# Nine warming matmuls instead of five, and the last stores cut at 80 rows and issued from two engines

## The chip, the core and the metric

The kernel runs on one NeuronCore of a Trainium2 chip. A core has engines with instruction streams of their own, which meet through semaphores: TensorE (PE; its weight loads are shown as PEld), VectorE (DVE), ScalarE (ACT), GpSimd (POOL) and SyncE (SP), which here only issues DMA. Sixteen DMA engines move data between HBM and the on-chip memory SBUF. Matmuls write PSUM, eight banks of 2 KB per partition, from which VectorE and ScalarE copy ("evict") results. The metric is device time of one execution in microseconds (us); lower is better.

## What is computed

The reference is a spectral layer followed by two gated feed-forward layers, on 2 x 3008 rows of 256 columns, all in float32:

```python
X = np.fft.rfft(x, axis=1)                      # x: (2, 3008, 256)
Yr = Xr @ w_r - Xi @ w_i + b_r
Yi = Xr @ w_i + Xi @ w_r + b_i
Yr, Yi = (np.sign(Y) * np.maximum(np.abs(Y) - 0.01, 0) for Y in (Yr, Yi))
y = np.fft.irfft(Yr + 1j * Yi, n=3008, axis=1)
x = y.reshape(6016, 256)
x = (sigmoid(x @ w_gate) * (x @ w_val)) @ w_out            # d_ff = 1536
x = (silu(x @ w2_gate) * (x @ w2_val)) @ w2_out            # d_ff = 1536
```

## The kernel before

**The whole.** The DFT of length 3008 = 47 x 64 is done as matmuls with tables, in stages: a first DFT over the 47 (94 rows with the two halves), a transposition, a second DFT over the 64, the complex product with w_r and w_i ("mix"), the shrinking, and the inverse in the same two steps. The two sequences (batches) are handled apart: batch 0 at the start of the kernel with everything kept on chip, batch 1 later, woven into the first feed-forward layer. The feed-forward layers run over 12 chunks of up to 512 rows and 12 blocks of 128 hidden columns; each float32 product there is made of three products of split operands (L636, L662). Weights come as float64 words and are split by VectorE and ScalarE as the kernel goes.

**The start.** `spectral_first` handles batch 0. Its function `load` (L288, L289) brings x in nine tiles `xr` of 94 partitions: two of 2 blocks ("tasks" `(0, 2)` and `(2, 2)`), seven of 4 blocks. Each tile takes two DMAs from SyncE, 80 rows and 14 rows. Six tiles have room at once, and the loads of the last three are issued when earlier tiles are used up. GpSimd fetches the table `f1f` (L293). Meanwhile VectorE clears a tile `idle`, and `warm(5)` issues five bf16 matmuls of 128 x 512 on it (L181), whose results nobody reads; each takes a PSUM tile of the pool `ps_b` (8 banks, tag "f"). Then the loop over the tasks: for each half d of the columns and each block a, one matmul of the tile's 94 x 128 block against `f1f` (L306, written into `p`); ScalarE (d = 0) and VectorE (d = 1) copy the bank into `zt`. With the last bank VectorE first converts the mixing weights `wmh` from `wraw` (L165, L166). PE takes its instructions in the order in which they are written, as does every other engine.

Then follows a loop over pairs of frequencies: `turn` transposes (L334, matmuls against the identity `eyes`) and copies out (ScalarE, L336), `forward` multiplies with a piece of the table `s2c` (L242), `mix` is 26 matmuls (L255), `inverse` uses pieces of `i1c` (L352). The pieces of `s2c` and `i1c` hold two turns each; the pieces 1 and 2 are loaded (L277) behind the first weights `raw` (L105 to L107).

**The queue of SyncE.** Nearly all loads and stores are issued by SyncE in program order. An issue also waits until the DMA that last used its semaphore has landed, so that about eight are under way. Around the change the order is: x tiles, `eyes` (L321), `s2c` piece 0, `wraw` (L154, L155), two bias rows (L156, L157), `f2s` (L158), `i1c` piece 0, weights, pieces 1 and 2.

**The end.** In the second layer, `turn_out` takes the finished chunk of up to 512 columns out of PSUM into `ot`, transposes it in blocks of 128 (L710) and copies each block into `ob` (ScalarE L716; VectorE L714 for the second block of the last chunk). Each row of `ob` is one row of the output, 1 KB. The rows of a block go to as many places as there are residues: a store (L721) ends where the block or a column of 94 rows of the output's layout ends. The last chunk has 384 rows and its stores are of 8, 94, 26 (first block), 68, 60 (second), 34 and 94 rows (third), all from SyncE. SyncE's last line, L860, waits for all DMAs to land.

The change touches `warm` and its call in `spectral_first`, and `turn_out`.

Of the kernel before, what the change touches and what calls it, by code (L numbers as in the profile page):

```python
# [9 lines left out]
F32 = mybir.dt.float32  # L10
# [10 lines left out]
PP = 32  # L21
NJ = 94
# [15 lines left out]
def tile_kernel(ctx, tc, x, w_r, w_i, b_r, b_i, wts, f1, f2, s2, i1, i1f, eye, one, out):  # L38
    nc = tc.nc
    P = 128  # L40
# [134 lines left out]

    idle = cp.tile([P, 512], BF16, name="idle")

    def warm(n):
        for i in range(n):
            pw = ps_b.tile([P, 512], F32, tag="f", name=f"warm{i}")  # L180
            nc.tensor.matmul(pw, idle[:, 0:P], idle, start=True, stop=True)  # L181


# [80 lines left out]
    def spectral_first(zz, ps):  # L264
# [3 lines left out]
        def bank(name):  # L268
            return ps.tile([P, 512], F32, tag="f", name=name)

        with tc.tile_pool(name="z0", bufs=1, reuse_waits="tile") as z0:
# [3 lines left out]
            def load_table2(c, t, src, into, bufs):  # L275
                into[c] = z0.tile([P, 4, P], F32, tag=t, bufs=bufs, name=f"{t}{c}")
                nc.sync.dma_start(into[c], src[:, 4 * c:4 * c + 4])  # L277

            tables = load_tables(z0)
            with tc.tile_pool(name="p1", bufs=1, reuse_waits="tile") as fp:  # L280
                xb = x[0].rearrange("(j p) c -> j p c", p=PP)
                xr = {}
                tasks = [(0, 2), (2, 2)] + [(p, 4) for p in range(4, PP, 4)]

                def load(t):
                    p0, n = tasks[t]
                    xr[t] = fp.tile([NJ, 4, 256], F32, tag="xr", bufs=6, name=f"xr0_{p0}")
                    nc.sync.dma_start(xr[t][0:80, :n], xb[0:80, p0:p0 + n, :])  # L288
                    nc.sync.dma_start(xr[t][80:94, :n], xb[80:94, p0:p0 + n, :])  # L289

                load(0)
                nc.gpsimd.memset(f1f[:, 96:P], 0.0)
                nc.gpsimd.dma_start(f1f[:, 0:96], f1[:, 2])  # L293
                for t in range(1, 6):
                    load(t)
                nc.gpsimd.memset(lam, -LAM)
                nc.scalar.activation(act, lam, AF.Sigmoid)
                nc.vector.memset(idle, 0.0)
                warm(5)
                next(tables)  # L300
                for t, (p0, n) in enumerate(tasks):
                    xt = xr.pop(t)
                    for d in range(2):
                        pt = bank(f"p1_0_{p0}_{d}")[:, :].rearrange("p (a c) -> p a c", c=P)
                        for a in range(n):
                            nc.tensor.matmul(pt[:, a], xt[:, a, d * P:(d + 1) * P], f1f,  # L306
                                             start=True, stop=True)
                        src = pt[:, 0:n, 0:96].rearrange("p a (q k) -> p k a q", q=4)
                        dst = zt[:, d, :, 4 * p0:4 * (p0 + n)].rearrange("p k (a q) -> p k a q", q=4)
                        if d and t == len(tasks) - 1:  # L310
                            next(tables)
                            nc.scalar.copy(dst[:, 0:KH // 2], src[:, 0:KH // 2])
                            nc.vector.tensor_copy(dst[:, KH // 2:], src[:, KH // 2:])
                        elif d:
                            nc.vector.tensor_copy(dst, src)
                        else:
                            nc.scalar.copy(dst, src)
                    if t + 6 < len(tasks):
                        load(t + 6)
                    if t == 3:  # L320
                        nc.sync.dma_start(eyes, eye)  # L321
                        load_table2(0, "s2c", s2, s2c, 3)
                        next(tables)
                        load_table2(0, "i1c", i1f, i1c, 4)
                        next(dec)
                next(tables)
# [258 lines left out]
    with tc.tile_pool(name="ps_b", bufs=8, space=PSUM) as ps_b:  # L585
        spectral_first(zz, ps_b)
        late_pools.append(ctx.enter_context(tc.tile_pool(name="wq", bufs=1, reuse_waits="tile")))
        mp = ctx.enter_context(tc.tile_pool(name="mp", bufs=2, reuse_waits="tile"))

        def split_x(m, ci):  # L590
            xs[m, ci] = tuple(mp.tile([P, 2, TC], F32R, tag=f"f{w}", bufs=RC, name=f"f{w}{m}_{ci}") for w in ("xh", "xl"))
            return xs[m, ci]

        def third_first():
            with tc.tile_pool(name="p3z", bufs=2, reuse_waits="tile") as fp:
                yield from stage3(0, fp, late_ps, zz, [split_x(0, c) for c in range(RC)], ps_b)
            pzs.close()

        third = third_first()
        next(third)  # L600
        fill(2)
        filled(2, nc.vector.tensor_copy)
# [48 lines left out]
    def project(m, ci, f, hh, hl):  # L651
        g0, tn = chunks[ci]
        wh, wl = blocks[m, f]
        first, last = runs[m, ci, f]
        if first:
            po[0] = [ps_o.tile([P, TC], F32, tag=f"o{d}", name=f"po{m}_{ci}_{d}") for d in range(2)]
        o = po[0]
        ops = [(d, w, v) for d in range(2) for w, v in ((wh, hh), (wh, hl), (wl, hh))]
        if (m, ci, f) == units[-1]:
            ops.sort(key=lambda op: op[2] is hl)  # L660
        for i, (d, w, v) in enumerate(ops):
            nc.tensor.matmul(o[d][:, :tn], w[:, 4 + d, :], v[:, :tn],  # L662
                             start=(first and d not in [q for q, _, _ in ops[:i]]),
                             stop=(last and d not in [q for q, _, _ in ops[i + 1:]]))
        if last and m:
            turned.append(turn_out(ci, o))
            next(turned[-1])
        if last and m == 0:
            drain(m, ci, f, o)
# [22 lines left out]
    def turn_out(ci, o):  # L692
        g0, tn = chunks[ci]
        end = ci == len(chunks) - 1
        ot = mp.tile([P, 2, TC], F32, tag="ot", bufs=1, name=f"ot{ci}")
        cut = 128 if end else tn
        for c in (slice(0, cut), slice(cut, tn)):
            if c.start < c.stop:
                nc.scalar.copy(ot[:, 0, c], o[0][:, c])
                nc.vector.tensor_copy(ot[:, 1, c], o[1][:, c])  # L700
        yield
        dst = out.rearrange("(b j p) c -> b p j c", b=B, p=PP)
        ob = mp.tile([P, 4, 256], F32, tag="ob", bufs=RC, name=f"ob{ci}")
        for j in range(0, tn, 256):
            pt = ps_f.tile([P, 2, 256], F32, tag="f", name=f"pt{ci}_{j}")
            js = [k for k in range(j, min(j + 256, tn), 128)]
            for a, k in enumerate(js):
                n = min(128, tn - k)
                for d in range(2):
                    nc.tensor.transpose(pt[:n, a, d * P:(d + 1) * P], ot[:, d, k:k + n], eyes)  # L710
            for a, k in enumerate(js):
                n = min(128, tn - k)
                if a and end:
                    nc.vector.tensor_copy(ob[:n, k // 128], pt[:n, a])  # L714
                else:
                    nc.scalar.copy(ob[:n, k // 128], pt[:n, a])  # L716
                r = 0
                while r < n:
                    pcol, jj = divmod(g0 + k + r, NJ)
                    step = min(n - r, NJ - jj)  # L720
                    nc.sync.dma_start(dst[pcol // PP, pcol % PP, jj:jj + step, :], ob[r:r + step, k // 128, :])  # L721
                    r += step
            yield


# [140 lines left out]
```

## Time and profile before

| | |
|---|---|
| median of 3 runs | 1378.81 us (1378.71 to 1380.22) |
| the profiled execution, its own time | 1378.57 us |
| its span, first to last instruction | 1376.5 us |
| PE busy | 1362.9 us, 99% |
| VectorE, ScalarE busy | 731.4 us (53%), 538.3 us (39%) |
| costliest line | L636, 3 x 1152 matmuls, 446.1 + 443.5 + 443.4 us |
| mean DMA rate | 55 GB/s; first of 40 slices 212 GB/s |

The span is what the trace covers; the time of an execution also holds what lies around it (here 2.07 us). A view of the trace gives start times in us from the span's start. "Busy" counts overlapping instructions of an engine once. In a timeline, consecutive instructions of one kind are merged into one row: start, time from the first's start to the last's end, and their number behind an x. SPq marks SyncE's issuing of DMAs: the row shows the issue, not the transfer. What an engine waited for stands behind "<-". DMA share is the busy time of the packets over that of 16 engines; it can exceed 1 where packets overlap. PEclk is the granted TensorE clock as a share of full speed.

### The profile page before, as it was taken

How to read it: one execution, taken by the hardware profiler on the slowest of the kernel's cores; microseconds unless marked ns; L12 is line 12 of the kernel's file. 1: busy time of each engine (PE TensorE's matmuls, PEld its weight loads, DVE VectorE, ACT ScalarE, POOL GpSimd, SP SyncE). 2: the span in 40 equal slices, each digit the busy share in tenths (PEclk: the TensorE clock that was granted, in tenths of full speed). 3: DMA queues.
4: the chain of work that ended last, by engine and by line, in shares of the span. 5: the costliest groups of instructions: out<-in, count | busy, mean ns of one | idle time of the engine just before them, and what ended most of it. 6: DMA issues, size and time to landing. Idle time of an engine off the chain costs nothing.

```text
span 1376.5 us, 16890 instructions
## 1 busy us (share of the span) xinstructions
PE 1362.9 (99%) x6784; PEld 1163.2 (85%) x6784; DVE 731.4 (53%) x1110; ACT 538.3 (39%) x941; POOL 11.0 (1%) x26
## 2 busy tenths in 40 slices
PE   9999999999999999999999999999999999999997
PEld 8998888888888888888889988888888888888896
DVE  1558984555334865633344755555455555555553
ACT  1655554444334443433333433333333333333332
POOL 1000000000000000000000000000000000000000
PEclk9999999999999999999999999999999999999999
DMA  8222442333332320200002101001101101100000
GB/s 212 67 78 83 147 127 82 108 108 103 100 110 80 100 77 0 77 31 31 1 27 77 50 1 31 24 7 32 31 1 31 32 0 31 31 6 26 27 16 12
DMA packets 57202, 76.35 MB, mean 55 GB/s; under 512 B 6084, under 2 KB 40615, under 8 KB 57124
## 3 DMA queue, kind: packets, MB, share of 16 engines
q1 hardware_dynamic: 54980, 71.69, 17.0%
q0 software_dynamic: 2144, 3.58, 1.3%
q8 instruction: 53, 0.87, 0.3%
q14 instruction: 25, 0.20, 0.0%
HBM read 51.53 MB, written 23.72 MB: 55 GB/s over the span
## 4 chain that ended last, share of the span: by engine, by line
PE 97%; DMA 1%; DVE 1%; ACT 0%; SPq 0%; issue 0%; ACTq 0%
PE pg L636 56%; PE po L662 28%; PE pm L255 5%; PE p L501 2%; PE p L306 2%; PE p L242 1%; PE pi L352 1%; PE pt L710 1%; PE p L219 1%; PE pi L448 1%; PE p L490 1%; PE pt L334 0%; DMA xr<-in_x_dram 0%; DMA xin<-xT 0%; PE p1e L577 0%; DVE yl L440 0%
## 5 line engine op out<-in xcount | busy, mean ns | idle before, releaser
L636 PE MATMUL pg<-fxh,wh 128*128 128x512 f32 (+1 forms) x1152 | 446.1, 387 | 0.0
L636 PE MATMUL pg<-fxl,wh 128*128 128x512 f32 (+1 forms) x1152 | 443.5, 385 | 0.0
L636 PE MATMUL pg<-fxh,wl 128*128 128x512 f32 (+1 forms) x1152 | 443.4, 385 | 0.0
L640 ACT ACTIVATE sg<-pg 128x512 f32<-128x512 f32 (+1 forms) x288 | 169.6, 589 | 362.2 <-PE pg L636 361.6
L644 DVE TENSOR_TENSOR h<-sg,pg 128x512 f32<-128x512 f32 (+1 forms) x288 | 194.5, 675 | 188.8 <-ACT sg L640 183.7
L647 ACT CAST hh<-h 128x512 fp32r<-128x512 f32 (+1 forms) x288 | 176.6, 613 | 300.2 <-DVE h L644 299.2
L649 DVE TENSOR_TENSOR hl<-h,hh 128x512 fp32r<-128x512 f32 (+1 forms) x288 | 195.9, 680 | 154.7 <-ACT hh L647 152.3
L636 PEld LDWEIGHTS pg<-fxh,wl 128*128 128x128 f32 x1152 | 216.2, 188 | 41.4
L636 PEld LDWEIGHTS pg<-fxh,wh 128*128 128x128 f32 x1152 | 216.5, 188 | 41.0 <-DVE fxl L512 0.2
L636 PEld LDWEIGHTS pg<-fxl,wh 128*128 128x128 f32 x1152 | 216.4, 188 | 39.9 <-issue 0.2
L662 PE MATMUL po<-hh,wh 128*128 128x512 f32 (+1 forms) x576 | 223.6, 388 | 0.3 <-ACT hh L647 0.3
L662 PE MATMUL po<-hh,wl 128*128 128x512 f32 (+1 forms) x576 | 221.9, 385 | 0.0
L662 PE MATMUL po<-hl,wh 128*128 128x512 f32 (+1 forms) x576 | 221.6, 385 | 0.0
L642 DVE TENSOR_TENSOR sg<-sg,pg 128x512 f32<-128x512 f32 (+1 forms) x144 | 97.4, 676 | 157.9 <-ACT sg L640 157.7
L662 PEld LDWEIGHTS po<-hh,wl 128*128 128x128 f32 x576 | 108.1, 188 | 20.8
L662 PEld LDWEIGHTS po<-hh,wh 128*128 128x128 f32 x576 | 108.2, 188 | 20.5 <-ACT hh L647 0.6
L662 PEld LDWEIGHTS po<-hl,wh 128*128 128x128 f32 x576 | 108.2, 188 | 20.2 <-DVE hl L649 0.2
L255 PE MATMUL pm<-wmh,Xh 128*128 128x256 f32 x192 | 54.2, 282 | 0.9 <-DVE Xl L234 0.9
L255 PE MATMUL pm<-wmh,Xl 128*128 128x256 f32 x192 | 53.7, 280 | 0.0
L255 PE MATMUL pm<-wml,Xh 128*128 128x256 f32 x192 | 53.7, 280 | 0.0
L625 DVE TENSOR_TENSOR fxl<-xin,fxh 128x512 fp32r<-128x512 f32 (+1 forms) x44 | 28.5, 677 | 19.4 <-ACT fxh L624 19.2
L255 PEld LDWEIGHTS pm<-wmh,Xh 128*128 128x128 f32 x192 | 36.2, 188 | 3.1 <-DVE Xl L234 2.7
(103 smaller groups left out, 854.2 us busy)
## 6 DMA issues: line engine op xcount, KB each, us to landing
raw<-in_moe_w_gate_dram SPq DMA_DIRECT2D x24, 256.0 KB
raw<-in_moe_w_val_dram SPq DMA_DIRECT2D x24, 256.0 KB
raw<-in_moe_w_out_dram SPq DMA_DIRECT2D x24, 256.0 KB
xin<-x2T SPq DMA_DIRECT2D x11, 512.0 KB
xT<-xo SPq DMA_DIRECT2D x26, 188.0 KB
x2T<-xo SPq DMA_DIRECT2D x9, 512.0 KB
xin<-xT SPq DMA_DIRECT2D x8, 512.0 KB
i1s<-in_tab_i_dram POOLq DMA_DIRECT2D x12, 256.0 KB, 4.2
```

Source lines behind the costliest of these rows:

```text
L219: nc.tensor.matmul(pt[c][:96], f1s[:, w, :], v, start=(i == 0), stop=(i == 2))
L255: nc.tensor.matmul(pm[:, k, :], a, w, start=(j == 0), stop=(j == len(ops) - 1))
L306: nc.tensor.matmul(pt[:, a], xt[:, a, d * P:(d + 1) * P], f1f, start=True, stop=True)
L501: nc.tensor.matmul(pt[:, d, q * NJ:(q + 1) * NJ], z[:, q, d * P:(d + 1) * P], f2s, start=True, stop=True)
L625: nc.vector.tensor_tensor(xl[:, k, :tn], xin[:, k, :tn], xh[:, k, :tn], op=ALU.subtract)
L636: nc.tensor.matmul(pg[:, s, :tn], w[:, 2 * s + k, :], v[:, k, :tn], start=(i == 0), stop=(i == 5))
L640: nc.scalar.activation(sg[:, :tn], pg[:, 0, :tn], AF.Sigmoid)
L642: nc.vector.tensor_tensor(sg[:, :tn], sg[:, :tn], pg[:, 0, :tn], op=ALU.mult)
L644: nc.vector.tensor_tensor(h[:, :tn], sg[:, :tn], pg[:, 1, :tn], op=ALU.mult)
L647: nc.scalar.copy(hh[:, :tn], h[:, :tn])
L649: nc.vector.tensor_tensor(hl[:, :tn], h[:, :tn], hh[:, :tn], op=ALU.subtract)
L662: nc.tensor.matmul(o[d][:, :tn], w[:, 4 + d, :], v[:, :tn], start=(first and d not in [q for q, _, _ in ops[:i]]), stop=(last and d not in ...
```

## The change

`warm` gets a second argument: the first `banks` matmuls take a new PSUM tile each, later ones write again into the last tile taken. The call becomes `warm(9, 5)`: nine matmuls, five tiles, as many tiles as before.

In `turn_out`, stores of the last chunk (`end`) take at most 80 rows each. A store is put into the list `late` and, outside the last chunk, taken out and issued from SyncE at once, as before. In the last chunk the stores of its first block (k = 0) and those of more than 60 rows are issued from SyncE at once; the others stay in the list and are issued from ScalarE at the end of the last block. With the sizes above that makes, in order, 8, 80, 14, 26, 68, 80 rows from SyncE and 60, 34, 14 rows from ScalarE.

```diff
--- before.py
+++ after.py
@@ -175,9 +175,10 @@
 
     idle = cp.tile([P, 512], BF16, name="idle")
 
-    def warm(n):
+    def warm(n, banks):
         for i in range(n):
-            pw = ps_b.tile([P, 512], F32, tag="f", name=f"warm{i}")
+            if i < banks:
+                pw = ps_b.tile([P, 512], F32, tag="f", name=f"warm{i}")
             nc.tensor.matmul(pw, idle[:, 0:P], idle, start=True, stop=True)
 
 
@@ -296,7 +297,7 @@
                 nc.gpsimd.memset(lam, -LAM)
                 nc.scalar.activation(act, lam, AF.Sigmoid)
                 nc.vector.memset(idle, 0.0)
-                warm(5)
+                warm(9, 5)
                 next(tables)
                 for t, (p0, n) in enumerate(tasks):
                     xt = xr.pop(t)
@@ -701,6 +702,7 @@
         yield
         dst = out.rearrange("(b j p) c -> b p j c", b=B, p=PP)
         ob = mp.tile([P, 4, 256], F32, tag="ob", bufs=RC, name=f"ob{ci}")
+        late = []
         for j in range(0, tn, 256):
             pt = ps_f.tile([P, 2, 256], F32, tag="f", name=f"pt{ci}_{j}")
             js = [k for k in range(j, min(j + 256, tn), 128)]
@@ -717,9 +719,14 @@
                 r = 0
                 while r < n:
                     pcol, jj = divmod(g0 + k + r, NJ)
-                    step = min(n - r, NJ - jj)
-                    nc.sync.dma_start(dst[pcol // PP, pcol % PP, jj:jj + step, :], ob[r:r + step, k // 128, :])
+                    step = min(n - r, NJ - jj, 80 if end else NJ)
+                    late.append((dst[pcol // PP, pcol % PP, jj:jj + step, :], ob[r:r + step, k // 128, :]))
+                    if not end or k == 0 or step > 60:
+                        nc.sync.dma_start(*late.pop())
                     r += step
+            if j + 256 >= tn:
+                for pair in late:
+                    nc.scalar.dma_start(*pair)
             yield
```

## Rows read from the trace of the kernel before

**Rows 1.** The page: PE's totals (busy us, share, instructions) and the granted clock in 40 slices
```profile
PE 1362.9 (99%) x6784; PEld 1163.2 (85%) x6784; DVE 731.4 (53%) x1110; ACT 538.3 (39%) x941; POOL 11.0 (1%) x26
...
PEclk9999999999999999999999999999999999999999
```

**Rows 2.** Chain of waits, 0 to 36 us: start us, us, what
```profile
8.28 24.25 PE p L306 x112
```

**Rows 3.** Timeline of PE, 22.7 to 41.8 us: start us, us, engine, line, what
```profile
22.71 9.81 PE L306 MATMUL p<-f1f,xr 94*128 94x128 f32 x45
32.31 0.42 PE L334 MATMUL pt<-eyes,zt 128*128 128x128 f32 x1
32.92 1.76 PE L334 MATMUL pt<-eyes,zt 128*128 128x128 f32 x7 [0.20 <-ACT zt L312]
34.50 1.67 PE L242 MATMUL p<-s2c,z 128*128 128x128 f32 x8
36.01 0.60 PE L334 MATMUL pt<-eyes,zt 128*128 128x128 f32 x4
36.44 1.06 PE L242 MATMUL p<-s2c,z 128*128 128x128 f32 x8
...
40.92 1.06 PE L242 MATMUL p<-s2c,z 128*128 128x128 f32 x8
```

**Rows 4.** Timeline of PE, 0 to 10 us; in brackets the idle time before
```profile
1.19 2.31 PE L181 MATMUL warm<-idle 128*128 128x512 bf16 x5 [1.19 <-DVE idle L298]
4.22 3.75 PE L306 MATMUL p<-f1f,xr 94*128 94x128 f32 x16 [0.71 <-DMA f1f<-in_tab_f_dram]
8.28 2.05 PE L306 MATMUL p<-f1f,xr 94*128 94x128 f32 x8 [0.31 <-DMA xr<-in_x_dram]
```

**Rows 5.** Timeline of the end, 1365 to 1377 us
```profile
1366.78 0.65 ACT L716 COPY ob<-pt 128x256 f32<-128x256 f32 x2 [0.75 <-PE pt L710]
1367.17 2.39 SPq L721 DMA_DIRECT2D out_dram<-ob  x7
1367.18 0.42 DVE L714 COPY ob<-pt 128x256 f32<-128x256 f32 x1 [0.89 <-ACT ob L716]
```

**Rows 6.** Windows: us, busy of each engine, then PEclk, DMA share, GB/s
```profile
8.00:12.00 4.00, 3.72 (x17) 3.75 (x18) 0.36 (x1) 0.48 (x1) 0.00 (x0) 1.00 1.21 240
25.00:30.00 5.00, 5.00 (x26) 5.00 (x25) 1.42 (x4) 0.48 (x1) 0.00 (x0) 1.00 0.98 337
30.00:35.00 5.00, 4.80 (x22) 4.18 (x22) 2.43 (x7) 1.67 (x4) 0.00 (x0) 1.00 0.03 12
1371.00:1373.00 2.00, 0.00 (x0) 0.00 (x0) 0.00 (x0) 0.00 (x0) 0.00 (x0) 0.50 0.15 43
1373.00:1375.00 2.00, 0.00 (x0) 0.00 (x0) 0.00 (x0) 0.00 (x0) 0.00 (x0) 0.50 0.13 47
1375.00:1376.50 1.50, 0.00 (x0) 0.00 (x0) 0.00 (x0) 0.00 (x0) 0.00 (x0) 0.50 0.00 0
```

**Rows 7.** Timeline of SyncE's issues, 11 to 26 us
```profile
14.16 0.36 SPq L321 DMA_DIRECT2D eyes<-in_tab_eye_dram  x1
...
15.65 0.38 SPq L154 DMA_DIRECT2D wraw<-in_w_r_dram  x1
...
17.45 0.64 SPq L156 DMA_DIRECT2D braw<-in_b_r_dram  x1
...
19.12 0.34 SPq L158 DMA_DIRECT2D f2s<-in_tab_f_dram  x1
...
23.53 0.43 SPq L277 DMA_DIRECT2D s2c<-in_tab_s_dram  x1
```

**Rows 8.** SyncE's waits, 0 to 32 us: total us, times, longest us
```profile
SPq L158 <- DMA xr<-in_x_dram: 0.5, 1, 0.5
```

**Rows 9.** DMA issues of the end, 1360 to 1377 us
```profile
out_dram<-ob SPq DMA_DIRECT2D x2, 94.0 KB
```

**Rows 10.** DMA issues of 0 to 30 us: KB each, us to landing
```profile
f1s<-in_tab_f_dram POOLq DMA_DIRECT2D x1, 70.5 KB, 9.3
```

## The prediction

> **What bounds the kernel now.** I read the page's totals first, then the chain of waits over the first 36 us, then TensorE's (PE's) timeline there, SyncE's issues beside it, and last the end. The totals say that PE is busy for 1362.9 of 1376.5 us [rows 1]: only 13.6 us are idle, and a change that fills idle time can't give more. But busy time is not work done. The chain spends 24.25 us, from 8.28 us on, in one line, the 112 recorded passes of the first DFT stage, `p` at L306 [rows 2]. Each matmul of 128 columns shows as two passes there.
>
> What the reader is to see next is the distance from one matmul to the next, which tells the clock's level here. In `p` 45 passes fill 22.71 to 32.31 us, where L334 begins: 9.60 / 45 = 0.213 us from start to start. The transposes L334 behind it take (34.50 - 32.92) / 7 = 0.226 us each, and from 36.01 us on the same transposes take (36.44 - 36.01) / 4 = 0.108 us [rows 3]. The factor of two is that between TensorE's levels of 1.2 and 2.4 GHz. So everything up to some 35 us ran at 1.2 GHz. The page's granted clock prints 9, full, from the first slice on [rows 1]; it does not show this, and the spacing decides. What PE did before: five warming matmuls in 2.31 us (512 columns at 1.2 GHz are 0.427 us), an idle gap of 0.71 us until f1f is there, and 28 us of `p` on 94 partitions, short of gaps [rows 4]. None of that raised the clock; it rose, between 34.5 and 36 us, in work on all 128 partitions with gaps in it [rows 3].
>
> Behind 36 us PE has hardly a gap until the end, so what is gained ahead of it reaches the end whole. At the end, the last seven stores are issued within 2.39 us from 1367.17 us [rows 5], yet the span ends at 1376.5. From 1371 to 1375 us the DMA share is 0.15 and 0.13 of 16 engines, so about two engines work and fourteen stand idle [rows 6].
>
> **The change part by part.**
>
> *Warming, if the clock rises.* Nine matmuls at 1.2 GHz start at 1.19 us and stream until 1.19 + 0.40 + 8 x 0.427 = 5.0 us, without the gap at 3.5 to 4.2: unbroken work on all 128 partitions, where the work that raised the clock later had gaps [rows 3]. Their banks are touched by PE alone, so none of them waits. I take it that the clock is up by the time `p` has been going a little. Then `p` is bound by its input. The third tile of x arrives at about 8.2 us [rows 4]. The later ones can be read off SyncE, whose issues wait for them: L321 at 14.16 us, L154 at 15.65, L156 at 17.45, L158 at 19.12 [rows 7, 8] stand for tiles six to nine of nine; the 14 rows that are loaded apart come some 0.2 us later. A tile of 16 passes takes 16 x 0.11 = 1.76 us instead of 16 x 0.213 = 3.41, about what a tile takes to arrive. From tile six: 14.4 + 4 x 1.76 = 21.4 us, against 32.3 now [rows 3]: **-10.9 us**. The exact moment of the rise hardly matters so long as it lies before 8.2 us.
>
> Behind it, sixteen passes of L334 and L242 that now run at half rate save 0.1 us each, 1.6 us; ScalarE's evictions between them hide part, so 0.5 to 1.6, and I take the middle, **-1.1**. What is late next is the tables: the third L242 group would come at 40.92 - 12.0 = 28.9 us [rows 3], and its table is issued at 23.53 us, first of the last four of 256 KB [rows 7]. DMA is full until 30 us and empty after [rows 6]; at 337 GB/s three tables take 2.3 us, so this one's bytes come at about 28 us and its landing is known a little later. A stall of 0 to 1.5 us; I take **+0.5**. The tables' bytes and the weights' beside them are moved no later than now. Sum **-11.5** (-12.5 to -9.5).
>
> *Warming, if it does not rise.* `p` starts 0.8 us later; the wait of 0.31 us for the third tile takes part of it back [rows 4]: **+0.4** (0.3 to 0.8).
>
> *Stores.* Chunks other than the last are issued as before. In the last, the two stores of 94 rows of 1 KB [rows 9] become 80 + 14. SyncE issues 8, 80, 14, 26, 68 and 80 rows; ScalarE, with nothing else left to do, issues 60, 34 and 14 after its last copy at 1367.4 us; its first waits for VectorE's copy until 1367.6 [rows 5]. From 1371 to 1375 us two engines move 45 KB per us, so each takes 0.045 us a row [rows 6]. A 94-row store leaves 47 rows to each of the two. As 80 rows over sixteen engines it leaves 5, and the 14 add one: the x loads, cut at 80 in the same way, hold the share at 1.21 [rows 6]. So 2 x (47 - 6) = 82 rows less on each of the two engines, 82 x 0.045 = **-3.7 us**. Bounds: at best the last issue decides, six of seven of 2.39 us, 1369.2 us, with the few tenths to its first packet and the 1.5 us that now lie between the last packet and the end [rows 6], which would be some -5; at worst nothing, if two engines have to carry it all the same. The stores of 34 and 68 rows stay as they are.
>
> ScalarE issues no DMA in this trace. Three issues cost it 1.0 us at SyncE's 0.34 each (2.39 / 7), up to 2 us at twice that: done at 1368.6 to 1369.6, no later than SyncE's own last. I take nothing for it.
>
> The Trainium skill, DMA: Bandwidth & Descriptors, "Rules for kernel authors", speaks against this part: spreading transfers over several issuing engines, or cutting one into parts by partitions, brings no bandwidth, as all run on the same sixteen DMA engines. By it the stores' term would be 0 and the sum 1367.3 us. The trace bears it out only where the sixteen are busy, and here two are.
>
> *Sum.* The profiled execution took 1378.57 us, 2.07 us more than its span and 0.24 us below the median of 1378.81. 1378.57 - 11.5 - 3.7 = 1363.4; with 0.2 for the median, **1363.6 us**.
>
> **The rivals.**
>
> *The clock stays low, or falls back.* For it: 24 us of gapless `p` have not raised it, and the five did not. Against: both were less than unbroken work on all partitions. It could also rise and fall again: at the upper level the first two tiles are done by 6.8 us and PE idles until 8.2 for the third [rows 4]; `p` then runs at 1.2 GHz as now. The only fall that the trace shows is after PE's last matmul, 0.50 from 1371 us on [rows 6]. Either way only the stores gain: 1378.8 + 0.4 - 3.7 = **1375.5 us**. Chance 0.30 (no rise 0.18, fall 0.12). The Trainium skill, TensorE: Matmul & The Clock Gate, "HAM oscillation", describes such a fall for a kernel whose PE waits for DMA between bursts; no run here shows one in the middle of a kernel.
>
> *The tail stays as long*, since the few engines carry the pieces too or the last landing has another cause: with the clock up 1367.3 us, chance 0.04; with the clock down 1379.2 us, no change, chance 0.03, which is also what it gives if the change does nothing that it says.
>
> *Slower: ScalarE's first DMA.* It has issued none before, and a queue used for the first time may answer slowly. The slowest landing among the early ones is 9.3 us (POOL's f1s, behind a full queue) [rows 10]. Its third, issued at 1369.0 where each issue takes twice SyncE's time, would land at 1378.3 instead of 1375.4, +2.9; with the clock down and 0.4 for the later `p`, 1378.8 + 0.4 + 2.9 = **1382.1 us** (with the clock up it would still be faster). From a landing of 6 us on it decides, from 8.8 us on measurably. Against it: DMA is nearly idle there. Chance 0.03.
>
> **How the numbers follow.** Forecast 0.60, rivals 0.30, 0.07 and 0.03. A measurement of this kernel can tell about 0.2%, 2.8 us, from no change, so faster begins below 1376.05. The forecast with its bounds spans 1360.5 to 1367; the first rival, 1374 to 1376.3, has 0.30 and must be in. So the range is 1360.5 to 1376.3, and 0.12 is left out. Faster: 0.60 + 0.04 + 0.7 of 0.30 (1375.5 is close to the bound) = 0.85. Same: 0.09 + 0.03 = 0.12. Slower 0.03. The likeliest case's own range is 1360.5 to 1367.
>
> **What would show it.** Right: passes of L306 at 0.11 us instead of 0.213, PE waiting for x at L306 again and again, L334 beginning near 21.4 us; at the end last packets near 1371.3 us of the old clock, DMA share well above 0.15 while they run. Wrong on the clock: L306 at 0.213 us from 8.3 us on, L334 near 32.7 us. Wrong on the stores: a stretch of several us at two engines, or a wait of SyncE's last line for ScalarE's stores. The forecast as a whole falls if the time is not below 1370 us.

## The result, and the profile after

The changed kernel takes 1364.33 us (median of nine runs, 1363.77 to 1376.53), the kernel before 1379.13 us (median of nine). The ratio is 0.9902, with a 95% interval of 0.9883 to 0.992. Eight of the nine runs lie between 1363.77 and 1366.31 us, one at 1376.53. In two of the experiments below (e4, e9) one run each had a mean granted clock near 0.56 and took about 2280 us; those two are left out of every number here. The profiled execution took 1366.31 us, 2 us more than the median; the waits in its middle are shown further down.

The page's totals, of which the first line stands here with the span, and the granted clock in 40 slices:

```profile
span 1364.3 us, 16902 instructions
...
PE 1352.1 (99%) x6788; PEld 1150.6 (84%) x6788; DVE 731.0 (54%) x1110; ACT 537.2 (39%) x941; POOL 11.0 (1%) x26
...
PEclk9999999999999999999999999999999999999999
```

PE is busy for 10.8 us less (1362.9 to 1352.1) with four more instructions [rows 1]. It did no less work; it did the same work at a higher clock. The clock row looks the same as before and again shows nothing of that.

PE's timeline from 0 to 36 us (start us, us, engine, line, what; in brackets the idle time before and what ended it), where the kernel's L306, L334 and L242 are now L307, L335 and L243:

```profile
1.19 4.02 PE L182 MATMUL warm<-idle 128*128 128x512 bf16 x9 [1.19 <-DVE idle L299]
5.00 2.67 PE L307 MATMUL p<-f1f,xr 94*128 94x128 f32 x16
8.50 13.45 PE L307 MATMUL p<-f1f,xr 94*128 94x128 f32 x112 [0.83 <-DMA xr<-in_x_dram]
21.79 0.27 PE L335 MATMUL pt<-eyes,zt 128*128 128x128 f32 x1
...
24.58 0.60 PE L335 MATMUL pt<-eyes,zt 128*128 128x128 f32 x4
...
30.23 1.13 PE L243 MATMUL p<-s2c,z 128*128 128x128 f32 x8 [0.57 <-DMA s2c<-in_tab_s_dram]
```

`p` begins at 5.00 us, without a gap behind the nine warming matmuls, where it waited 0.71 us before [rows 4]. (A row's end is modelled, so the warming row reaches 5.21.) The first 16 passes take 2.67 us instead of 3.75, so the clock rose inside them; the 112 behind take 13.45 us instead of 24.25 [rows 2]. L335 begins at 21.79 us, where L334 began at 32.31 [rows 3]. PE now waits 0.83 us for the third tile of x, and 0.57 us for the table of the third L243 group, which comes at 30.23 us instead of 40.92.

The chain of waits over the same stretch (start us, us, what) has changed its kind:

```profile
2.50 5.59 DMA xr<-in_x_dram
...
8.17 7.74 DMA xr<-in_x_dram
...
16.36 6.38 DMA wraw<-in_w_i_dram
...
24.20 5.90 DMA s2c<-in_tab_s_dram
```

Loads stand in the chain of the first 30 us now, where `p` did [rows 2]. It ends in PE's wait for the table at 30.23 us, so a still faster PE would bring nothing there, and an earlier table no more than the wait of 0.57 us. `p` itself is close to both bounds, the arrival of x and PE's own pace. Its sixth tile begins at 14.57 us, and the 64 passes from there to L335 take 7.22 us, 0.113 us each; that is about PE's own pace at the high clock, which e10 below shows: 112 passes from 15.06 to 27.57 us without a wait, 0.112 us each.

PE's waits over the whole span (total us, times, longest us) show where some of the gain is given back:

```profile
PE pm L256 <- DVE Xl L235: 1.5, 1, 1.5
PE p L502 <- DMA z<-scr: 1.2, 1, 1.2
```

The first is 0.9 us in the kernel before, the second has no counterpart there. Both lie far behind the start, at 253 and 349 us.

The end, in the timeline and in windows (us; busy us of PE, PEld, DVE, ACT, POOL; PEclk; DMA share; GB/s):

```profile
1358.69 0.65 ACT L718 COPY ob<-pt 128x256 f32<-128x256 f32 x2 [0.74 <-PE pt L712]
1359.09 2.27 SPq L725 DMA_DIRECT2D out_dram<-ob  x6
...
1359.37 1.41 ACTq L729 DMA_DIRECT2D out_dram<-ob  x3
```

```profile
1360.00:1361.00 1.00, 0.00 (x0) 0.00 (x0) 0.00 (x0) 0.00 (x0) 0.00 (x0) 1.00 0.48 142
1361.00:1362.00 1.00, 0.00 (x0) 0.00 (x0) 0.00 (x0) 0.00 (x0) 0.00 (x0) 0.79 0.46 128
1362.00:1363.00 1.00, 0.00 (x0) 0.00 (x0) 0.00 (x0) 0.00 (x0) 0.00 (x0) 0.50 0.36 115
1363.00:1364.30 1.30, 0.00 (x0) 0.00 (x0) 0.00 (x0) 0.00 (x0) 0.00 (x0) 0.50 0.00 0
```

ScalarE's last copies begin at 1358.69 us, 8.1 us earlier than in the kernel before [rows 5]. From there to the span's end (called the tail from here on) it takes 5.6 us, where it took 1376.5 - 1366.78 = 9.7. SyncE issues six stores in 2.27 us, ScalarE three in 1.41 (0.47 each, waits included). ScalarE's come in the order 34, 60, 14 rows and not 60, 34, 14; by the sizes in the trace its first issue, at 1359.37 us, is of 34 rows. The stretch of 4 us at a share of 0.13 to 0.15 [rows 6] is gone; the share stays at 0.36 to 0.48 until the last packets.

So of the 12.2 us between the two spans (1376.5 - 1364.3), 8.1 come from before the last copies and 4.1 from the tail.

### The profile page after: what moved, and what is told of

It is laid out like the page before. It is cut to its first block, busy times and chain, and to the rows that moved or that the text cites. A ratio compares the mean times of both kernels' runs of the same rounds, so it can differ in the third digit from the quotient of the medians.

```text
span 1364.3 us, 16902 instructions
## 1 busy us (share of the span) xinstructions
PE 1352.1 (99%) x6788; PEld 1150.6 (84%) x6788; DVE 731.0 (54%) x1110; ACT 537.2 (39%) x941; POOL 11.0 (1%) x26
## 4 chain that ended last, share of the span: by engine, by line
PE 91%; DMA 4%; DVE 2%; ACT 1%; SPq 1%; issue 0%; DVEq 0%; ACTq 0%
PE pg L637 53%; PE po L663 27%; PE pm L256 5%; PE p L502 2%; PE p L243 1%; DMA raw<-in_moe_w_out_dram 1%; DMA xr<-in_x_dram 1%; PE pi L353 1%; DMA xin<-xT 1%; PE pt L712 1%; PE p L220 1%; PE p L491 1%; PE pi L449 0%; DMA wraw<-in_w_i_dram 0%; DMA s2c<-in_tab_s_dram 0%
## 5 line engine op out<-in xcount | busy, mean ns | idle before, releaser
L256 PE MATMUL pm<-wmh,Xh 128*128 128x256 f32 x192 | 54.2, 282 | 1.5 <-DVE Xl L235 1.5
L256 PE MATMUL pm<-wmh,Xl 128*128 128x256 f32 x192 | 53.7, 280 | 0.0
L256 PE MATMUL pm<-wml,Xh 128*128 128x256 f32 x192 | 53.7, 280 | 0.0
L256 PEld LDWEIGHTS pm<-wmh,Xh 128*128 128x128 f32 x192 | 36.2, 188 | 3.6 <-DVE Xl L235 3.2
```

The lines of the kernel that those rows point to most:

```text
L256: nc.tensor.matmul(pm[:, k, :], a, w, start=(j == 0), stop=(j == len(ops) - 1))
```

## The experiments

Each kernel was timed beside the kernel before, and the ratio is to that. Rows carry the line numbers of the run that they come from: where an edit adds lines they stand a little further (e10's L310 is L307). A run's tail comes from its one profiled execution. The fences of edits show the lines that differ, without those around them; a longer gap is marked by dots. The theory: the clock's early rise brings some 11 us, the shorter tail some 4, each without the other. The rivals were that one of the two carries it all, that the warming matmuls are paid for, and that the tail is a matter of the issuing engine.

| run | edit | median us (runs) | ratio, 95% interval | tail us |
|---|---|---|---|---|
| e1 | warming alone | 1369.08 (4) | 0.9921 (0.9906 to 0.9936) | 9.9 |
| e2 | stores alone | 1376.11 (6) | 0.9971 (0.9959 to 0.9982) | 5.6 |
| e3 | stores cut, all from SyncE | 1364.76 (4) | 0.9887 (0.987 to 0.9903) | 6.4 |
| e4 | stores not cut, two from ScalarE | 1369.11 (3) | 0.9913 (0.9897 to 0.993) | 9.6 |
| e5 | seven warming matmuls | 1374.87 (12) | 0.9941 (0.9917 to 0.9965) | 5.7 |
| e6 | twelve warming matmuls | 1364.39 (4) | 0.9889 (0.9876 to 0.9901) | 5.7 |
| e7 | nine, and four in the wait for x | 1364.39 (4) | 0.989 (0.9877 to 0.9903) | 5.7 |
| e8 | nine on 94 partitions | 1376.07 (6) | 0.9973 (0.9961 to 0.9984) | 5.7 |
| e9 | third tile of x late | 1383.03 (7) | 1.0026 (1.0015 to 1.0038) | 5.7 |
| e10 | the same, wait filled | 1369.99 (3) | 0.9936 (0.9914 to 0.9959) | 5.7 |
| e11 | stores cut at 47 rows | 1376.5 (1) | | 16.6 |
| e12 | twelve, 68 and 34 rows cut | 1364.46 (4) | 0.9896 (0.9879 to 0.9912) | 5.4 |

### One part of the change without the other: e1 and e2

```diff
 e1 = the kernel before, and
-    def warm(n):
+    def warm(n, banks):
 ...
-                warm(5)
+                warm(9, 5)
 e2 = the changed kernel, and
-                warm(9, 5)
+                warm(5, 5)
```

> Nine warming matmuls, stores as before. Theory (the clock's early rise is worth some 11 us, the stores some 4): 1368 to 1369 us in nearly all runs, L306 at 0.11 us per pass from some 6.5 us on, the tail from PE's last matmul to the end 9.7 us as before. Rival (the stores carry the gain, or both are needed): over 1375 us.

> Five warming matmuls, stores as changed. Theory: the clock stays low until the transposes, 1374.5 to 1375.5 us, the tail some 5.5 us instead of 9.7. Rival (the tail belongs to ScalarE's issues and ends no earlier without them in the right place, or the gain was one of the clock alone): 1378 to 1380 us.

e1 keeps the long tail of 9.9 us and is 0.8% faster; e2 has the short tail and is 0.3% faster. The two reductions, 0.79% and 0.29%, make 1.08%, against 0.98% (0.8 to 1.17) for the change as a whole: the parts add up. e2's median lies 0.6 us above the expected range; its batch's kernel before stood at 1380.52 us, 1.4 above the other batch. In e2's trace PE's timeline has `p` at the low clock to the end:

```profile
8.28 24.23 PE L307 MATMUL p<-f1f,xr 94*128 94x128 f32 x112 [0.22 <-DMA xr<-in_x_dram]
32.30 0.42 PE L335 MATMUL pt<-eyes,zt 128*128 128x128 f32 x1
```

These are the 24.25 us and 32.31 us of before [rows 2, 3].

### What in the stores shortens the tail: e3, e4, e11, e12

```diff
 e3: all from SyncE
-                    if not end or k == 0 or step > 60:
+                    if True:
 e4: not cut
-                    step = min(n - r, NJ - jj, 80 if end else NJ)
+                    step = min(n - r, NJ - jj, NJ)
 e11 = e3, cut at 47 rows
-                    step = min(n - r, NJ - jj, 80 if end else NJ)
+                    step = min(n - r, NJ - jj, 47 if end else NJ)
```

> Nine warming matmuls; the last stores cut at 80 rows, all nine issued from SyncE in the order of the rows. Theory (it is the 94 rows that lie on two DMA engines): most of the tail's gain stays; SyncE has three more issues of some 0.34 us behind its six, so the last one comes 1.0 us later and the tail is 5.9 to 6.7 us instead of 5.5; 1364.5 to 1365.5 us. Rival (the second issuing engine brings the gain): tail over 8 us, 1367 to 1368.5 us.

> Nine warming matmuls; the last stores not cut, those of 60 and 34 rows issued from ScalarE. Theory: two stores of 94 rows still put 47 rows each on two DMA engines, tail 8.5 to 9.7 us, 1367 to 1368.5 us. Rival (the second issuing engine brings the gain): tail near 5.5 to 6.5 us, 1364 to 1365.5 us.

> Nine warming matmuls; the last stores cut at 47 rows instead of 80 (94 = 47 + 47), all issued from SyncE. Theory (the number of rows of a store decides over how many DMA engines it spreads, and 47 does worse than 94): a long stretch at a DMA share below 0.13, tail over 9 us. Rival (shorter stores are faster, whatever their number of rows): tail 7 us or less, about as with the cut at 80 from SyncE alone.

The cut alone (e3) brings the tail to 6.4 us, the second issuer alone (e4) to 9.6, next to nothing. Both together bring 5.6. Thus in the traces the cut is worth 3.3 of the 4.1 us and ScalarE's issues, where the cut has made room for them, 0.8. The medians show the cut as well (1364.76 us in e3 against 1369.08 in e1) and nothing for the second issuer alone (1369.11 in e4); one of e4's three runs took 1366.68 us, and why is not known. They don't resolve the 0.8 us. e3's timeline shows what they save, nine issues from one engine in 3.38 us against 2.27:

```profile
1357.10 3.38 SPq L725 DMA_DIRECT2D out_dram<-ob  x9
```

In e4 two issuers are at work, and the windows still have the long stretch near two of sixteen engines (a share of 0.125):

```profile
1362.00:1364.00 2.00, 0.00 (x0) 0.00 (x0) 0.00 (x0) 0.00 (x0) 0.00 (x0) 0.50 0.18 63
1364.00:1366.00 2.00, 0.00 (x0) 0.00 (x0) 0.00 (x0) 0.00 (x0) 0.00 (x0) 0.50 0.11 39
```

e11, of which there is one run, decides what the cut does. It makes the stores shorter than the change does, and the tail is 16.6 us, the longest of all. Its issues and windows:

```profile
1358.56 8.11 SPq L725 DMA_DIRECT2D out_dram<-ob  x11
```

```profile
1366.00:1368.00 2.00, 0.00 (x0) 0.00 (x0) 0.00 (x0) 0.00 (x0) 0.00 (x0) 0.50 0.07 24
1368.00:1370.00 2.00, 0.00 (x0) 0.00 (x0) 0.00 (x0) 0.00 (x0) 0.00 (x0) 0.50 0.07 24
1370.00:1372.00 2.00, 0.00 (x0) 0.00 (x0) 0.00 (x0) 0.00 (x0) 0.00 (x0) 0.50 0.07 24
1372.00:1375.00 3.00, 0.00 (x0) 0.00 (x0) 0.00 (x0) 0.00 (x0) 0.00 (x0) 0.50 0.03 12
```

A share of 0.07 is one engine of sixteen (0.0625), which moves 24 KB per us. The eleven issues are drawn out too, but they are over by 1366.67 us, and the one engine works on for some 6 us. So a store of 94 rows lies on two engines, one of 47 rows on one, and one of 80 on many (the share is 0.36 to 0.48 in the changed kernel): the number of rows decides, not how short the store is. The Trainium skill, DMA: Bandwidth & Descriptors, "Why a DMA increments its semaphore by 16 and not by 1", gives the rule: the largest number up to 16 that divides the count of rows. The trace agrees, with 0.13 at 94 rows [rows 6] and 0.07 at 47. Of its "Rules for kernel authors", which the prediction put against the change, e4 agrees with the one on several issuers. The one on two transfers to disjoint halves of the partitions gives as its reason that both halves run on all sixteen engines; here the uncut store ran on two, and e3 shows the cut to pay.

e12 cuts what was left on few engines, and takes twelve warming matmuls:

```diff
-                warm(9, 5)
+                warm(12, 5)
                     step = min(n - r, NJ - jj, 80 if end else NJ)
+                    step -= step % 16 if end and step in (34, 68) else 0
```

> Twelve warming matmuls, and of the last stores those of 68 and 34 rows cut once more, into 64 + 4 and 32 + 2; SyncE issues 8, 80, 14, 26, 64 and 80 rows, ScalarE 4, 60, 32, 2 and 14. Theory (rows that lie on two or four DMA engines still set a part of the tail): tail 5.3 to 5.6 us instead of 5.9, in all 1363.3 to 1364.5 us, no run near 1376. Rival (the tail is now set by the issues and the landing of the last store): tail 5.8 us or more, as ScalarE has two more issues of some 0.4 us, 1364 to 1365 us.

The tail shrinks by 0.3 us against e6, which has twelve warming matmuls too, to 5.4, though ScalarE issues five stores:

```profile
1356.60 0.65 ACT L718 COPY ob<-pt 128x256 f32<-128x256 f32 x2 [0.75 <-PE pt L712]
1356.99 2.72 SPq L726 DMA_DIRECT2D out_dram<-ob  x6
...
1357.27 2.27 ACTq L730 DMA_DIRECT2D out_dram<-ob  x5
```

That speaks for a small part that rows on few engines still had in it, but it rests on one trace of each, and the medians don't resolve it: 1364.46 against 1364.39 in e6.

### How many warming matmuls: e5 and e6

```diff
-                warm(9, 5)
+                warm(7, 5)      (e6: warm(12, 5))
```

> Seven warming matmuls (they end at some 4.15 us, where f1f arrives, so the gap before L306 is gone as well), stores as changed. Theory (it is the length of the unbroken warming work that lifts the clock): the clock rises early in a part of the runs only, so the runs fall into two groups, near 1364 and near 1375.5 us. Rival (closing the gap ahead of L306 is enough): all near 1364 us. Second rival (nothing short of nine lifts it): all near 1375.5 us.

> Twelve warming matmuls, stores as changed. Theory: the clock rises in every run; the three more take 1.3 us at the low level or 0.6 at the high one, and L306 waits for the third tile of x until some 8.4 us anyway, so no time is lost: 1363.5 to 1365 us. Rival (warming is paid for in full): 1364.9 to 1366 us.

With seven, twelve runs scatter: four at 1363.2 to 1364.6 us, one at 1369.2, seven at 1373.7 to 1377.9. With twelve, all four lie within 1363.87 to 1364.74. In the profiled execution seven leave no gap ahead of L307 either, and by the scatter closing the gap isn't enough. The profiled execution of e5 shows a third course, which the expectation did not name. PE's timeline, and windows with the granted clock as the third column from the right:

```profile
4.22 2.02 PE L307 MATMUL p<-f1f,xr 94*128 94x128 f32 x16
8.61 2.02 PE L307 MATMUL p<-f1f,xr 94*128 94x128 f32 x16 [2.37 <-DMA xr<-in_x_dram]
10.80 20.78 PE L307 MATMUL p<-f1f,xr 94*128 94x128 f32 x96 [0.16 <-DMA xr<-in_x_dram]
...
35.11 0.60 PE L335 MATMUL pt<-eyes,zt 128*128 128x128 f32 x4
```

```profile
4.00:8.00 4.00, 2.25 (x17) 1.86 (x16) 0.72 (x2) 0.64 (x2) 1.44 (x3) 1.00 0.89 208
8.00:12.00 4.00, 3.23 (x22) 3.10 (x23) 0.56 (x1) 0.48 (x1) 0.00 (x0) 0.86 1.21 244
12.00:20.00 8.00, 8.00 (x39) 8.00 (x39) 1.12 (x2) 1.29 (x3) 0.00 (x0) 0.50 1.01 249
20.00:30.00 10.00, 10.00 (x49) 10.00 (x48) 2.34 (x5) 1.20 (x4) 0.00 (x0) 0.50 0.93 292
...
36.00:42.00 6.00, 6.00 (x54) 5.96 (x53) 3.97 (x8) 4.54 (x9) 0.00 (x0) 1.00 0.29 90
```

The clock is up for the first 16 passes (2.02 us) and the next 16; PE waits 2.37 us for x between them; then the clock falls to 0.50, level 1.2 GHz, and stays there for the rest of `p` (96 passes in 20.78 us) until L335 and L243 have been at work. This is the fall that the prediction's first rival described, seen in a trace. By the 0.86 of the second window it comes near 10.9 us, 2.3 us after PE took up work again, so this trace alone doesn't tie it to the wait; e9 and e10 test that on a longer one. In two of e5's runs, at 1373.74 and 1376.88 us, the mean granted clock is 0.990 and 0.989 where all others have 0.998 or more; the other five of the seven read 0.999 like e2 and e8, so that in them the early rise was missing altogether. The changed kernel's one run at 1376.53 us has 0.991. As the records count the low clock only behind the first rise, 0.009 of 1374.5 us at half rate are 2 x 12.4 = 25 us of low clock, 2.7 of them at the end, so that run too saw the clock rise and fall again, by its mean clock alone, as it has no trace.

In e6 PE's timeline has no gap in the first 48 passes:

```profile
1.19 5.30 PE L182 MATMUL warm<-idle 128*128 128x512 bf16 x12 [1.19 <-DVE idle L299]
6.29 5.97 PE L307 MATMUL p<-f1f,xr 94*128 94x128 f32 x48
...
21.61 0.27 PE L335 MATMUL pt<-eyes,zt 128*128 128x128 f32 x1
```

Three more matmuls begin `p` 1.3 us later and L335 not at all later (21.61 against 21.79): they lie in the wait for x.

### The fall: e7, e9 and e10

```diff
 e7 and e10: warm takes pw as a third argument and returns it
-                warm(9, 5)
+                pw = warm(9, 5)
 ...
+                    if t == 2:
+                        warm(4, 0, pw)      (e10: warm(36, 0, pw))
                     xt = xr.pop(t)
 e9 and e10: the third tile is loaded last of six
-                for t in range(1, 6):
+                for t in (1, 3, 4, 5, 2):
                     load(t)
```

> Nine warming matmuls, and four more between the second and the third tile of x, where L306 now waits 0.8 us or more for the third. Theory (the one run of nine near 1376.5 us is one in which the clock rose and fell back in that wait): none near 1376, all 1363.5 to 1365 us, mean granted clock 0.998 or more in each. Rival (that run never saw the early rise): such a run can still turn up; its mean clock is then near 0.999 like that of the kernel before.

> The kernel as changed, but the third tile of x is loaded behind the fourth to sixth, so that L306 waits for it until some 14 us instead of 8.4, with PE idle for 7 us from some 7.4 us on. Theory (an idle wait of PE lets the clock fall, and L306 on 94 partitions does not lift it again): granted clock 0.5 in the wait and through the rest of L306, whose passes stand 0.213 us apart; L335 begins near 38 us; 1380 to 1383 us, slower than the kernel before. Rival (once up, the clock stays up through such a wait): passes 0.11 us apart, L335 near 26 us, 1368 to 1371 us.

> As the run before, with 36 warming matmuls in front of the third tile, which fill the wait (36 x 0.213 = 7.7 us). Theory: no fall, granted clock 1.00, L335 near 26 us, 1368 to 1371 us, with the same late loads. Rival (the late loads themselves cost the time, or the clock falls for another reason): as slow as the run before.

e9 lengthens the wait to 7.69 us, and the clock falls in every run: seven runs between 1381.99 and 1384.35 us with mean clocks of 0.986 to 0.988, slower than the kernel before. PE's timeline and windows:

```profile
5.00 2.80 PE L307 MATMUL p<-f1f,xr 94*128 94x128 f32 x16
15.49 24.23 PE L307 MATMUL p<-f1f,xr 94*128 94x128 f32 x112 [7.69 <-DMA xr<-in_x_dram]
39.52 0.42 PE L335 MATMUL pt<-eyes,zt 128*128 128x128 f32 x1
```

```profile
7.00:11.00 4.00, 0.81 (x8) 0.61 (x6) 0.66 (x2) 0.32 (x1) 0.00 (x0) 0.90 1.14 254
11.00:15.00 4.00, 0.00 (x0) 0.00 (x0) 0.00 (x0) 0.00 (x0) 0.00 (x0) 0.50 1.04 238
...
20.00:30.00 10.00, 10.00 (x49) 10.00 (x49) 1.59 (x3) 1.44 (x3) 0.00 (x0) 0.50 0.91 264
```

The clock goes from 1.00 to 0.50 in the idle stretch (0.90 on the average of the first window, 0.50 in all of the second), and 24 us of `p` without a gap don't raise it. In e10 the loads are just as late, 36 warming matmuls fill the wait, and `p` runs at the high clock:

```profile
7.29 7.93 PE L182 MATMUL warm<-idle 128*128 128x512 bf16 x36
15.06 12.67 PE L310 MATMUL p<-f1f,xr 94*128 94x128 f32 x112
27.57 0.27 PE L338 MATMUL pt<-eyes,zt 128*128 128x128 f32 x1
```

13.0 us lie between the two medians, from matmuls whose results nobody reads. So it is PE's idleness in the wait that lets the clock fall; late loads alone cost 5.6 us (1369.99 against 1364.39 of e7). The Trainium skill, TensorE: Matmul & The Clock Gate, "HAM oscillation", describes such a fall in DMA waits; e9 agrees, with 0.50 from within a wait of 7.69 us on.

In e7 no run is near 1376, but four runs can't show that a case of one in nine is gone: it would stay out of four runs more often than not. It stayed out of all twelve runs of e1, e3, e4 and e11 too, which have the nine matmuls and no filling: it is one run of 21. e7's own runs are compatible with the theory, e9 and e10 carry it.

### Which work lifts the clock: e8

```diff
-            nc.tensor.matmul(pw, idle[:, 0:P], idle, start=True, stop=True)
+            nc.tensor.matmul(pw, idle[0:NJ, 0:P], idle[0:NJ], start=True, stop=True)
```

> Nine warming matmuls on 94 of 128 partitions, for as long as the nine on 128, stores as changed. Theory (work on 94 partitions does not lift the clock, which is why 24 us of L306 did not): no early rise, L306 at 0.213 us per pass, 1375 to 1376.5 us. Rival (any unbroken bf16 work of that length lifts it, and L306 fails for another reason): near 1364 us.

All six runs lie between 1374.69 and 1376.98 us. PE's timeline:

```profile
1.19 4.02 PE L182 MATMUL warm<-idle 94*128 94x512 bf16 x9 [1.19 <-DVE idle L299]
5.00 27.59 PE L307 MATMUL p<-f1f,xr 94*128 94x128 f32 x128
...
36.38 0.60 PE L335 MATMUL pt<-eyes,zt 128*128 128x128 f32 x4
```

The nine matmuls take the same 4.02 us, on 94 partitions, `p` follows without a gap, and all 128 passes stay 0.213 us apart; the clock rises only between 34.6 and 36.4 us, in the transposes and matmuls on 128 partitions behind, as before [rows 3]. The profile of before had shown that 24 us of `p` don't lift the clock; in e8 the nine bf16 matmuls of 512 columns don't either, and all that sets them apart from those of the changed kernel is 94 partitions for 128. That `p` is float32 is not the reason: L334 and L242, in which the clock rose, are too [rows 3].

## Why the prediction was right

1363.6 us were forecast with 0.60, and 1364.33 came. Step by step, against the profiled execution:

- **The clock rises with nine warming matmuls.** Right (e1, e8). It was up within the first 16 passes of `p`. No row of before could show that nine are enough; the prediction took it, with 0.18 against. e5 shows how near the edge it was: with two fewer the rise was missing in five of twelve runs, and in two more the clock fell again. So there was luck in it.
- **`p` is then bound by x: -10.9.** Right within 0.4 us; L335 begins 10.5 us earlier. The sixth tile begins at 14.57 us for the 14.4 worked out, and the four tiles from there take 7.22 us for 4 x 1.76 = 7.04. The sign named for it, PE waiting for x again and again, is weak: one wait of 0.83 us, and 0.1 to 0.2 us more at each of the fourth to sixth tiles.
- **The sixteen passes behind: -1.1.** The gain grows from 10.5 us at L335 (21.79 for 32.31) to 11.4 at the third turn's (24.58 for 36.01 [rows 3]): -0.9.
- **The tables come late: +0.5.** Right; a wait of 0.57 us at the place named, and the gain at L243 is 40.92 - 30.23 = 10.7 us instead of 11.4, so +0.7.
- **"What is gained ahead of it reaches the end whole."** This step was mis-sized. Of 10.7 us at 30 us the last copies show 8.1: 2.6 us are lost between, 1.2 at L502 in a wait for a load, 0.6 more than before at L256, the rest in small pieces. In other kernels with the early rise the last copies begin 10.7 us (e7), 10.1 (e6, e3), 9.2 (e4) or 7.7 (e1) earlier than in the profile of before, so that the loss differs from one execution to the next; the median, 2 us under the profiled execution, fits a small loss. The wait at L502 is 0.2 to 1.4 us in the traces with the early rise, but for e10, which has none; where the clock stayed low or fell back it is 0 to 0.5. What brings it was not tried and stays open.
- **The stores: -3.7**, from 82 rows less on each of two engines. Right in kind, by e4 and e11, and 0.4 us short: the tail lost 4.1. Of these the cut brings 3.3, within 0.4 of the sum, and ScalarE's issues, which I took for nothing, 0.8.
- **ScalarE's issues at 0.34 to 0.68 us each.** 0.47. The prediction let the first wait for VectorE's copy; it is the store of 34 rows, and the one of 60 that waits comes second.

The sum came within 0.7 us partly because misses offset each other: at 30 us the start had gained 10.7 us of the 11.5 forecast, and the tail 4.1 for 3.7. The ends of the likeliest case's range, 1360.5 and 1367, do not follow from the bounds given: -12.5 and -5 make 1361.3, -9.5 and 0 make 1369.3. No result came near enough for that to matter.

The first rival came true in one run of nine (and in none of the twelve others that warm in the same way): 1376.53 us against the 1375.5 worked out for it, and by its mean clock it was the fall (0.12) and not the missing rise (0.18). That the clock is up "by the time `p` has been going a little" held in all nine by their mean clocks, and that it stays up was what one run broke; a median hides that. The rivals on the tail and on ScalarE's first DMA were wrong: in a tail of 5.6 us there is no room for a slow first landing.

What the experiments add for this kernel: twelve warming matmuls (e6) cost nothing against nine, as they lie in the wait for x, and leave PE no wait for the third tile. The clock stayed up in all eight runs with twelve (e6, e12); against one fall in 21 runs with nine, that shows no difference, and the median is the same.

## What to carry to other kernels

A PE that is 99% busy can still run at half speed: divide a stretch by the number of its matmuls and compare it with the same instruction elsewhere before you believe it is bound by work. Matmuls whose results nobody reads pay where PE would otherwise wait and its clock would stay low or fall, ahead of the first stage (e1) and in a long wait behind it (e10); in a wait that the clock outlasts they bring nothing (e7, the same median). Count how many fit until the data arrives. And look at the row counts of the last stores: 94, which of the numbers up to 16 only 1 and 2 divide, put them on two of sixteen engines, and 80 + 14 was 3 us faster than 94.

## What was not expected of the hardware

- The granted clock of the profile begins with its first recorded change. e8 ran at the low level for 36 us and its mean clock reads 0.999; e5, whose clock rose first and then fell, reads 0.990. So a low mean tells of a fall and says nothing of a late rise.
- A stage can hold a clock that it did not raise. The 112 passes of `p` on 94 partitions kept 2.4 GHz for 13.45 us in the changed kernel, and kept 1.2 GHz for 24.23 us in e9. It does not always hold it: in e5 the clock fell near 10.9 us while `p` was at work, after a wait of 2.37 us.
- Stores cut into halves took longer than the whole: with at most 47 rows instead of 94 the tail was 16.6 us against 9.9 (e11, e1), both from SyncE alone.
